# Attention prologue of a three-layer kernel: GpSimd starts after the ranking, VectorE subtracts for two heads at once, score tile 0 stands between the mask rows

## The chip, the cores and the metric

The kernel runs on one core of a Trainium2 chip. The metric is the time of one execution on the device, in microseconds (us). A profile is one further execution with the hardware profiler on; its times below count from the start of its span.

## The reference

Three layers in a row: clustered attention (batch 2, 8 heads, 768 positions, 64 columns a head, 16 clusters a head), then two feed-forward layers on its result. The change touches only the start of the attention.

```python
q_assign = argmax(einsum('bhsd,hcd->bhsc', q_n, c_n))   # 16 clusters a head, the first maximum wins
k_assign = argmax(einsum('bhsd,hcd->bhsc', k_n, c_n))
mask = q_assign[:, :, :, None] == k_assign[:, :, None, :]
scores = where(mask, (q @ k.T) / 8, -1e9)
attn = softmax(scores)                                   # then attn @ v
x = attention, heads side by side                        # 1536 x 512
h = x @ w_in;  g = rational(h);  y = g @ w_out           # 2048 hidden columns
logits = y @ phi; soft mixture of 8 experts (w1, relu, w2) over 32 slots
```

## The kernel before, in words

**Pairs and tiles.** Heads are handled in 8 pairs; a pair lies on 128 partitions, 64 for each head. A score tile is 128 queries of one head against all 768 keys, so a pair has 12 tiles and the attention 96. Tile u belongs to pair u // 12, and head u % 2. For each head of a pair four operands of 128 x 768 exist, `q1`, `q2`, `k1`, `k2` (the profile prints them as q and k): the inputs are split into a high part and a low rest (`qh` and `ql`, `ka` and `kb`) for accuracy, and 16 rows of `q2` and `k2` hold the cluster as one-hot mask rows. A tile is the sum of a first pass (`q1` against `k1`) and a second pass (`q2` against `k2`), each in two column halves (`a1_mm`, L361 and L362).

**The loop.** Slots n from -2 on; every engine runs its instructions in the order in which they are written, and a table `plan` puts each step of a pair's preparation, of a weight decoder and of the normalisation into a slot. Slot n does, for tile n + 2, the matmuls (`a1_mm`) and VectorE's pass that scales and takes the row minimum (`a1_neg`, L370); ScalarE's exponential (`a1_exp`, L374) follows one slot later. For tile n TensorE transposes (`turn`, L385) and ScalarE copies (`turned`, L391); matmuls with `v` follow six slots later (L398). In this text neg(u), exp(u), turn(u) and copy(u) are these steps of tile u. There is one PSUM buffer for the scores of tiles and one for the transposed ones.

**Preparation of a pair.** Cluster scores (`scores`, L240), scaled by the centroids' inverse norms `rn` (`scaled`, L245), transposed (`scT`, L250), then the ranking on VectorE: maximum (`mx`, L255), comparison (L257), first maximum by rank (L266, L268, L270), which leaves the one-hot tile `eq`. For pairs from 1 on GpSimd splits k (`ksplit`, tiles ka, kb) and q (`qsplit`, qh, ql), and SP copies the parts and the mask rows (`nh`, from ScalarE's `masks`, L280) into the operands by DMA: `mspread` is eight such DMAs (L288), `qspreads` six (L324).

**Pair 0** (`first_pair`) has its own code, before the loop. `front` writes high parts with ScalarE (q) and GpSimd (k), rests with VectorE and GpSimd, moves halves of them between partitions by DMA (`q_over`, `k_over`), and makes mask rows with TensorE's transposes of `eq` (`rows`, L182), VectorE (`q_rows`, L186) and ScalarE (`k_rows`, L190). `idle(n)` is n matmuls on zeros that nobody reads. `start` loads the centroids (`cP` for the norms, `cT` for the scores), q and k of pair 0 in two column halves, and the constants, and computes `rn` in a dozen small steps on VectorE with one on GpSimd (L495).

**Weight decoder.** `w_in` and `w_out` come as 64-bit numbers and are decoded beside the attention (`decode_steps`: load, `bits` L519 and L520, `expo` on ScalarE, `mant` L526, `sign` L530, `value` L535 and `parts` on GpSimd, `store`), at the slots in `DEC`. The feed-forward layers follow after the last tile; expert weights (`wt`) are loaded by SP as their buffers come free.

Of the kernel before, what the change touches and what calls it, by code (L numbers as in the profile page):

```python
# [52 lines left out]
def tile_kernel(ctx, tc, qT, kT, v, cenT, cenP, consts, constsb, ab, w_in, w_out, phi, w1, w2, out, dbg=None):  # L53
# [60 lines left out]
    PREP1 = (-2, 0, 0, 1, 1, 2, 1, 2, 3, 3, 4, 5, 6, 2, 3, 5, 7)  # L114
# [28 lines left out]
    def first_pair(r, o, f):  # L143
# [40 lines left out]
        def q_rows(h, c):
            a = slice(AT[h], AT[h] + 16)
            DVE.tensor_scalar(o[h]["q2"][a, halves[c]], ms["q", h][a, halves[c]], -1.0, None, ALU.add)  # L186

        def k_rows(h):
            a = slice(AT[h], AT[h] + 16)
            ACT.activation(o[h]["k2"][a, :], ms["k", h][a, 0:S], AF.Copy, scale=BIG)  # L190

        def front():
            f["scores"]()
            q_high(0)
            q_low(0, DVE)
# [17 lines left out]
            for h in range(2):  # L213
                rows("k", h)
                k_rows(h)
                rows("q", h)
                q_rows(h, 0)
# [3 lines left out]
                (0, "D", lambda: q_rows(0, 1)),  # L221
                (1, "D", lambda: q_rows(1, 1))]
# [128 lines left out]
    def a1_mm(u):  # L351
# [115 lines left out]
    def start():  # L467
        DVE.memset(zero, 0.0)
        idle(9)
        ACT.dma_start(cP, cenP)  # L470
        ACT.dma_start(cT, cenT)
        nc.scalar.preload_act_table_set("natural_log_exp_and_others")

        for n in "kq":
            raws.setdefault(0, {})[n] = raw_p.tile([128, S], F32, tag="raw" + n, name="raw" + n, bufs=2)
        for c in range(2):
            w = slice(c * HS, (c + 1) * HS)
            for n in "kq":
                SP.dma_start(raws[0][n][:, w], (kT if n == "k" else qT)[0, 0][:, w])
# [15 lines left out]
        POOL.tensor_scalar(t, r, 1e-6, 1.0, ALU.add, ALU.mult)  # L495
# [852 lines left out]
```

## Time and profile before

| | |
|---|---|
| time, median of 3 runs | 520.5 us (520.29 to 522.15) |
| the profiled execution | 519.72 us, of which 517.9 us are its span |
| TensorE busy | 499.2 us, 96% of the span, mean granted clock 0.994 |
| VectorE, ScalarE, GpSimd busy | 406.1, 366.2 and 280.3 us |
| span 0 to 16 us | TensorE busy 11.06, VectorE 9.65, ScalarE 7.04, GpSimd 11.38 us |
| span 48 to 265 us | TensorE busy 214.08 of 217 us |

The profiled execution is 1.8 us longer than its span, for what lies around it, and 0.8 us under the median. Busy shares are averages over stages: the attention fills the first half of the span, the two feed-forward layers the second.

### The profile page before, as it was taken

To read this page: it belongs to the slowest core of one execution; us is meant where nothing else is said; L and a number is where in the kernel's file an instruction comes from. 1 tells how busy PE (TensorE), PEld (TensorE's weight loads), DVE (VectorE), ACT (ScalarE), POOL (GpSimd) and SP (SyncE) were. 2 spreads that over 40 slices of the span, in tenths; PEclk is the share of its full clock that TensorE was granted. 3 is DMA by queue.
4 is the path that set the end of the run, shared out by engine and by line. 5 is a ranking of instruction groups with operands and counts; after the bars stand their busy time and mean duration, and the time that the engine had idled before them with its cause. 6 is when DMAs were issued, how large, how long until landed. Compare 5 with 4: busy or idle time off the path is not lost.

```text
span 517.9 us, 9816 instructions
## 1 busy us (share of the span) xinstructions
PE 499.2 (96%) x3439; PEld 336.2 (65%) x3439; DVE 406.1 (78%) x747; ACT 366.2 (71%) x653; POOL 280.3 (54%) x321
## 2 busy tenths in 40 slices
PE   6899999999999999999999999999999999999994
PEld 2656566666666666567666877777777767764462
DVE  6698899798998988988642999999799996985021
ACT  4577888788788887778773888879588786771111
POOL 6444876549676496665423855555355544641000
PEclk9899999999999999999999999999999999999999
DMA  6849889797986869773401767766567765799997
GB/s 198 243 135 271 259 219 320 220 259 216 265 292 175 285 203 295 240 212 130 164 1 64 259 232 264 276 226 224 185 223 253 263 216 195 271 352 378 422 414 307
DMA packets 43984, 124.61 MB, mean 241 GB/s; under 512 B 6944, under 2 KB 8992, under 8 KB 39328
## 3 DMA queue, kind: packets, MB, share of 16 engines
q1 hardware_dynamic: 43504, 123.54, 71.2%
q8 instruction: 27, 0.44, 0.4%
q10 hardware_dynamic: 432, 0.46, 0.3%
q14 instruction: 21, 0.17, 0.1%
HBM read 89.56 MB, written 15.73 MB: 203 GB/s over the span
## 4 chain that ended last, share of the span: by engine, by line
PE 70%; DVE 12%; DMA 9%; ACT 6%; issue 2%; POOL 1%; SPq 0%; ACTq 0%; POOLq 0%; DVEq 0%
PE sT L385 10%; PE av L398 10%; PE h L771 9%; PE h L774 9%; PE h L772 9%; DMA wt<-w 7%; PE s L361 5%; PE s L362 5%; DVE e L370 4%; PE gt L818 4%; ACT e L374 2%; ACT eT L391 2%; PE l L830 2%; PE dg L892 1%; DMA raw<-w_out 1%
## 5 line engine op out<-in xcount | busy, mean ns | idle before, releaser
L374 ACT ACTIVATE e<-e,nv 128x768 f32<-128x768 f32 x96 | 89.9, 937 | 44.1 <-DVE e L370 37.5
L370 DVE TENSOR_SCALAR_CACHE_REDUCE e<-s 128x768 f32<-128x768 f32 x96 | 91.5, 954 | 30.0 <-PE s L362 23.4
L385 PEld LDWEIGHTS sT<-cst,e 128*128 128x128 f32 x576 | 61.5, 141 | 45.5 <-ACT eT L391 24.6
L385 PE MATMUL sT<-cst,e 128*128 128x128 f32 x576 | 83.5, 281 | 2.2 <-ACT eT L391 1.7
L391 ACT COPY eT<-sT 128x768 f32<-128x768 f32 x96 | 75.4, 786 | 7.4 <-PE sT L385 6.8
L771 PE MATMUL h<-xh,w 128*128 128x512 f32 x192 | 80.6, 420 | 0.0
L535 POOL TENSOR_TENSOR w<-mh,ex 128x516 f32<-128x516 f32 x32 | 41.3, 1290 | 66.4 <-DVE ex L530 54.8
L398 PE MATMUL av<-eT,vt 128*64 128x384 f32 x384 | 77.2, 504 | 0.0
L788 POOL TENSOR_SCALAR q<-u,babs 128x512 f32<-128x512 f32 x47 | 36.5, 776 | 73.6 <-ACT u L786 73.6
L361 PE MATMUL s<-k,q 128*128 128x384 f32 x192 | 73.6, 384 | 2.1 <-DVE e L370 1.9
L772 PE MATMUL h<-xl,w 128*128 128x512 f32 x192 | 75.3, 392 | 0.0
L362 PE MATMUL s<-k,q 80*128 80x384 f32 x192 | 64.9, 338 | 0.0
L790 POOL TENSOR_TENSOR q<-q,u 128x512 f32<-128x512 f32 x47 | 61.0, 1299 | 3.8
L774 PE MATMUL h<-xh,w 128*128 128x512 f32 x192 | 52.9, 396 | 0.0
L786 ACT ACTIVATE u<-h 128x512 f32<-128x512 f32 x47 | 27.9, 594 | 27.2 <-PE h L774 23.6
L771 PEld LDWEIGHTS h<-xh,w 128*128 128x128 f32 x192 | 36.1, 188 | 16.3 <-DVE r L804 3.4
L789 DVE TENSOR_TENSOR p<-p,h 128x512 f32<-128x512 f32 x47 | 32.1, 683 | 15.0 <-ACT p L787 14.9
L774 PEld LDWEIGHTS h<-xh,w 128*128 128x128 f32 x192 | 35.9, 188 | 8.6 <-DMA w<-w_in 0.2
L361 PEld LDWEIGHTS s<-k,q 128*128 128x128 f32 x192 | 36.5, 190 | 6.6 <-DVE e L370 5.7
L772 PEld LDWEIGHTS h<-xl,w 128*128 128x128 f32 x192 | 36.2, 189 | 6.7 <-issue 0.5
L796 ACT ACTIVATE r<-q,epsc 128x512 f32<-128x512 f32 x47 | 32.8, 697 | 9.5 <-POOL q L790 7.5
L398 PEld LDWEIGHTS av<-eT,vt 128*64 128x64 f32 x384 | 21.4, 135 | 24.4 <-issue 22.7
(203 smaller groups left out, 956.3 us busy)
## 6 DMA issues: line engine op xcount, KB each, us to landing
wt<-w SPq DMA_DIRECT2D x32, 1024.0 KB, 8.2
w<-w_in SPq DMA_DIRECT2D x96, 256.0 KB, 3.3
raw<-w_in SPq DMA_DIRECT2D x16, 512.0 KB, 4.8
raw<-w_out SPq DMA_DIRECT2D x16, 512.0 KB, 4.7
w_in<-w SPq DMA_DIRECT2D x16, 512.0 KB, 4.4
k<-ka SPq DMA_DIRECT2D x28, 192.0 KB, 4.9
q<-qh SPq DMA_DIRECT2D x28, 192.0 KB, 4.7
w_out<-w SPq DMA_DIRECT2D x16, 256.0 KB, 4.9
```

What stands on the lines that cost most here:

```text
L361: PE.matmul(ps[:, c, 0:HS], o["q1"][:, it], o["k1"][:, w], start=True, stop=False)
L362: PE.matmul(ps[:, c, 0:HS], o["q2"][rows, it], o["k2"][rows, w], start=False, stop=True)
L370: DVE.tensor_scalar(e, s1s.pop(u)[:, :, 0:HS], -(D ** -0.5), None, ALU.mult, ALU.min, accum_out=nvs[g][:, rest:rest + 1])
L374: ACT.activation(es[u], es[u], AF.Exp, scale=-1.0, bias=nvs[g][:, rest:rest + 1], accum_out=sums[g][:, rest:rest + 1])
L385: PE.transpose(ps[:, j // 3, j % 3 * 128:(j % 3 + 1) * 128], e[:, j, :], ident)
L391: ACT.copy(dst, eTp.pop(u)[:, :, 0:HS].rearrange("p c (j t) -> p c j t", j=3))
L398: PE.matmul(av[g][64 * h:64 * h + 64, 0:HS], vs[g // 2][:, h, j, :], eTs[g][:, h, j, :], start=(j == 0), stop=(j == 5))
L535: POOL.tensor_tensor(w.rearrange("p (r n) -> p r n", r=3), hold["mh"].bitcast(F32), hold["ex"].bitcast(F32), ALU.mult)
L771: PE.matmul(h, wh[:, c, :], xh[t][:, c, :], start=(c == 0), stop=False)
L772: PE.matmul(h, wh[:, c, :], xl[t][:, c, :], start=False, stop=False)
L774: PE.matmul(h, wl[:, c, :], xh[t][:, c, :], start=False, stop=(c == NCC - 1))
L790: POOL.tensor_tensor(q, q, u, ALU.mult)
```

## The change

In `front`, ScalarE writes the high parts of q (first half) and of all of k to whole 128-partition tiles `qh` and `ka`; VectorE makes the rests `ql` and `kb` for both heads in one instruction each; ScalarE then writes the heads' own parts, and SP also carries `kb` to `k2` by DMA (`k_low`). GpSimd's first instruction after its memsets is a copy of one element of the finished `eq` (`gate`), so its work on q's second half starts after the ranking. The mask rows are made for q's first half only, before tile 0; its second half follows in slot 0. Tile 0's and tile 1's passes stand apart, between mask rows and pair 1's cluster scores. In `start`, SP issues the centroids `cP` first, ScalarE issues `cT` and q, SP k, and the GpSimd step of `rn` moves to VectorE. Pair 1's steps move in the slots (`PREP1`), the first decoder starts two slots earlier (`DEC`), and six of the idle matmuls go.

```diff
-    PREP1 = (-2, 0, 0, 1, 1, 2, 1, 2, 3, 3, 4, 5, 6, 2, 3, 5, 7)
+    PREP1 = (-1, 0, 1, 1, 2, 1, 3, 4, 4, 5, 5, 6, 2, 3, 6, 7)
...
+        def q_high(c, copy):
+            copy(hold["qh"][:, halves[c]], r["q"][:, halves[c]])
         def q_low(c, engine):
-            for h in range(2):
-                at = own[h], halves[c]
-                engine.tensor_tensor(hold["ql"][at], r["q"][at], o[h]["q1"][at].bitcast(F32), ALU.subtract)
+            w = halves[c]
+            engine.tensor_tensor(hold["ql"][:, w], r["q"][:, w], hold["qh"][:, w].bitcast(F32), ALU.subtract)
+        def q_own(n, h, c, copy):
+            copy(o[h][n][own[h], halves[c]], r["q"][own[h], halves[c]])
-        def k_high(h):
-            POOL.tensor_scalar(o[h]["k1"][own[h], :], r["k"][own[h], :], 1.0, 1.0, ALU.mult, ALU.mult)
+        def k_own(h):
+            ACT.copy(o[h]["k1"][own[h], :], r["k"][own[h], :])
         def k_low(h):
-            POOL.tensor_tensor(o[h]["k2"][own[h], :], r["k"][own[h], :], o[h]["k1"][own[h], :].bitcast(F32), ALU.subtract)
+            SP.dma_start(o[h]["k2"][own[h], :].bitcast(F32), hold["kb"][own[h], :].bitcast(F32))
...
-        def front():
+        def front(nxt):
             f["scores"]()
-            q_high(0)
+            q_high(0, ACT.copy)
+            ACT.copy(hold["ka"], r["k"])
             q_low(0, DVE)
-            k_high(0)
-            k_high(1)
+            DVE.tensor_tensor(hold["kb"], r["k"], hold["ka"].bitcast(F32), ALU.subtract)
+            k_over(0)
+            k_over(1)
             q_over(0, 0)
-            k_over(0)
+            k_low(0)
             q_over(1, 0)
-            k_over(1)
+            k_low(1)
             f["scaled"]()
             f["scT"]()
             f["best"](0)
             f["best"](1)
             for i in range(3):
                 f["first"](i)
-            q_high(1)
-            k_low(0)
-            k_low(1)
+            for h in range(2):
+                q_own("q1", h, 0, ACT.copy)
+                k_own(h)
+                q_own("q2", h, 0, ACT.copy)
+            pool_copy(s2_p.tile([128, 1], F32, tag="gate", name="gate"), hold["eq"][:, 2, 7, 15:16])
+            q_high(1, pool_copy)
             q_low(1, POOL)
+            for n in ("q1", "q2"):
+                for h in range(2):
+                    q_own(n, h, 1, pool_copy)
             idle(11)
-            for h in range(2):
-                rows("k", h)
-                k_rows(h)
-                rows("q", h)
-                q_rows(h, 0)
+            rows("q", 0, (0,))
+            rows("k", 0, (0, 1))
+            q_rows(0, 0)
+            k_rows(0)
+            a1_mm(0, (0,))
+            rows("q", 1, (0,))
+            q_rows(1, 0)
+            a1_mm(0, (1,))
+            rows("k", 1, (0, 1))
+            k_rows(1)
+            a1_mm(1, (0,))
+            nxt()
+            a1_mm(1, (1,))
...
-        idle(9)
-        ACT.dma_start(cP, cenP)
+        idle(8)
+        SP.dma_start(cP, cenP)
...
-            for n in "kq":
-                SP.dma_start(raws[0][n][:, w], (kT if n == "k" else qT)[0, 0][:, w])
+            SP.dma_start(raws[0]["k"][:, w], kT[0, 0][:, w])
+            ACT.dma_start(raws[0]["q"][:, w], qT[0, 0][:, w])
...
-        POOL.tensor_scalar(t, r, 1e-6, 1.0, ALU.add, ALU.mult)
+        DVE.tensor_scalar(t, r, 1e-6, None, ALU.add)
...
-    DEC = [2 + 53 * i // 20 for i in range(2 * NF)]
+    DEC = [2 * (i > 0) + 53 * i // 20 for i in range(2 * NF)]
...
-            if n > 0 or n == -LEAD:
+            if n >= 0:
                 a1_mm(pend)
             a1_neg(pend)
-            if n < 0:
-
-                a1_mm(n + 1 + LEAD)
...
-        if n < 6 and n != -1:
-            idle(2 if n < 0 else 3)
+        if 0 < n < 6:
+            idle(3)
```

GpSimd, from its last memset to the first work for pair 1. Before, it makes the norm's step, then high parts and rests of pair 0 (rawk and rawq are the inputs, k_0_0 and q_0_0 operands of head 0, k_0_1 and q_0_1 of head 1):

```order
L495 TENSOR_SCALAR pc<-pc 128x4
L167 TENSOR_SCALAR k_0_0_118<-rawk 64x768
L167 TENSOR_SCALAR k_0_1_122<-rawk 64x768
L170 TENSOR_TENSOR k_0_0_119<-rawk,k_0_0_118 64x768
L170 TENSOR_TENSOR k_0_1_123<-rawk,k_0_1_122 64x768
L161 TENSOR_TENSOR ql<-rawq,q_0_0_116 64x384
L161 TENSOR_TENSOR ql<-rawq,q_0_1_120 64x384
L293 TENSOR_SCALAR ka<-rawk 128x768
```

Now the copy out of `eq` stands first, and only q's second half follows before pair 1's ka:

```order
L177 TENSOR_SCALAR gate<-eq 128x1
L177 TENSOR_SCALAR qh<-rawq 128x384
L159 TENSOR_TENSOR ql<-rawq,qh 128x384
L177 TENSOR_SCALAR q_0_0_116<-rawq 64x384
L177 TENSOR_SCALAR q_0_1_120<-rawq 64x384
L177 TENSOR_SCALAR q_0_0_117<-rawq 64x384
L177 TENSOR_SCALAR q_0_1_121<-rawq 64x384
L318 TENSOR_SCALAR ka<-rawk 128x768
```

All of k's work has left this place, and nothing of GpSimd's runs while VectorE ranks.

TensorE, from the last mask row of before to the transposes of tile 1 (s is a score tile, mf the cluster scores, sT the transposed tile, rest the idle matmuls; rows that repeat are left out):

```order
L182 MATMUL mb<-cb,eq 16x128
L361 MATMUL s_276<-k_0_0_118,q_0_0_116 128x384
L362 MATMUL s_276<-k_0_0_119,q_0_0_117 128x384
...
L361 MATMUL s_285<-k_0_1_122,q_0_1_120 128x384
L362 MATMUL s_285<-k_0_1_123,q_0_1_121 128x384
...
L240 MATMUL mf<-rawq,cT 32x384
...
L465 MATMUL rest<-zero 128x512
...
L361 MATMUL s_302<-k_0_0_118,q_0_0_116 128x384
...
L385 MATMUL sT<-cst,e 128x128 x6
L250 MATMUL mf<-cst,sc 128x128 x3
```

Now, from the first score pass on:

```order
L392 MATMUL s_262<-k_0_0_118,q_0_0_116 128x384 x2
...
L187 MATMUL mb<-cb,eq 16x128
...
L390 MATMUL s_262<-k_0_0_119,q_0_0_117 128x384 x2
...
L392 MATMUL s_278<-k_0_1_122,q_0_1_120 128x384 x2
L265 MATMUL mf<-rawq,cT 32x384
...
L390 MATMUL s_278<-k_0_1_123,q_0_1_121 128x384 x2
L418 MATMUL sT<-cst,e 128x128 x6
L392 MATMUL s_315<-k_0_0_118,q_0_0_116 128x384
```

Tile 0's two passes now enclose q's rows of head 1, tile 1's enclose pair 1's cluster scores, and tile 2 (s_302 before, s_315 now) follows turn(0) in place of preceding it.

ScalarE, from tile 0's exponential on (sc is pair 1's scaled cluster scores, eT the copy of a transposed tile). Before:

```order
L374 ACTIVATE e,ssum<-e,nv 128x768 x2
L391 COPY eT<-sT 128x6x128
L245 ACTIVATE sc<-mf,pc 128x384
L374 ACTIVATE e,ssum<-e,nv 128x768
L391 COPY eT<-sT 128x6x128
```

Now:

```order
L407 ACTIVATE e,ssum<-e,nv 128x768
L270 ACTIVATE sc<-mf,pc 128x384
L407 ACTIVATE e,ssum<-e,nv 128x768
L424 COPY eT<-sT 128x6x128
L407 ACTIVATE e,ssum<-e,nv 128x768
```

The scaling for pair 1 has moved from behind copy(0) to ahead of exp(1). On SP's queue the store of the first decoded weights, which stood between pair 1's eight mask-row DMAs and its six q DMAs, now stands ahead of both. From tile 6 on VectorE's instructions stand in the same order in both kernels, and so do the other engines' from a few tiles later to the end.

## Rows read from the trace of the kernel before

**Rows 1.** The chain of waits near the span's end: start, duration in us, what.
```profile
472.49 15.93 DMA wt<-w
```
**Rows 2.** Timeline of SP's queue near the end: start, us, engine, line, operation, tiles.
```profile
446.19 42.63 SPq L751 DMA_DIRECT2D wt<-w  x21
```
**Rows 3.** Timeline of the prologue, all engines; brackets: idle before, and what ended it.
```profile
7.25 0.20 POOL L495 TENSOR_SCALAR pc<-pc 128x4 f32<-128x4 f32 x1 [3.54 <-DVE pc L494]
...
7.57 2.28 DVE L161 TENSOR_TENSOR ql<-rawq,q 64x384 fp32r<-64x384 f32 x2
7.75 0.58 ACT L245 ACTIVATE sc<-mf,pc 128x384 f32<-128x384 f32 x1 [1.11 <-DVE pc L496]
8.23 2.09 ACT L154 CAST q<-rawq 64x384 fp32r<-64x384 f32 x4
...
8.77 2.54 PE L465 MATMUL rest<-zero 128*128 128x512 bf16 x11
...
9.53 3.87 POOL L170 TENSOR_TENSOR k<-rawk,k 64x768 fp32r<-64x768 f32 x2
9.89 0.56 DVE L255 TENSOR_REDUCE mx<-mf 128x24 f32<-128x384 f32 x1
...
11.07 0.66 DVE L266 TENSOR_TENSOR eq<-eq,cb 128x384 bf16<-128x384 bf16 x1
...
12.35 1.46 DVE L270 TENSOR_TENSOR eq<-eq,mr 128x384 bf16<-128x384 bf16 x1
...
13.86 2.49 PE L182 MATMUL mb<-cb,eq 128*16 128x128 bf16 x24 [2.55 <-DVE eq L270]
...
14.71 1.69 ACT L190 ACTIVATE k<-mb 16x768 fp32r<-16x768 bf16 x2 [4.39 <-PE mb L182]
...
17.64 0.96 DVE L370 TENSOR_SCALAR_CACHE_REDUCE e<-s 128x768 f32<-128x768 f32 x1 [0.69 <-PE s L362]
...
18.52 0.95 DVE L370 TENSOR_SCALAR_CACHE_REDUCE e<-s 128x768 f32<-128x768 f32 x1
```
**Rows 4.** The same timeline later, while GpSimd has nothing to do.
```profile
25.91 0.35 DVE L266 TENSOR_TENSOR eq<-eq,cb 128x384 bf16<-128x384 bf16 x1
...
28.84 0.55 DVE L270 TENSOR_TENSOR eq<-eq,mr 128x384 bf16<-128x384 bf16 x1
...
29.80 0.34 PE L275 MATMUL mb<-cb,eq 128*128 128x128 bf16 x3
...
32.11 1.29 POOL L535 TENSOR_TENSOR w<-mh,ex 128x516 f32<-128x516 f32 x1 [13.40 <-DVE ex L530]
```
**Rows 5.** Groups by line of VectorE, 17 to 34 us: busy us, mean ns.
```profile
L370 DVE TENSOR_SCALAR_CACHE_REDUCE e<-s 128x768 f32<-128x768 f32 x7 | 6.6, 954 | 1.4 <-PE s L362 1.0 <-ACT eT L391 0.4
L519 DVE TENSOR_SCALAR ex<-raw 128x516 int32<-128x516 int32 x2 | 1.4, 682 | 0.0
...
L186 DVE TENSOR_SCALAR q<-mb 16x384 fp32r<-16x384 bf16 x2 | 1.1, 552 | 0.1
```
**Rows 6.** Windows: busy of five engines, then granted clock, DMA share, GB/s.
```profile
13.00:13.50 0.50, 0.00 (x0) 0.00 (x0) 0.50 (x1) 0.00 (x0) 0.42 (x2) 1.00 0.83 318
...
14.00:14.50 0.50, 0.50 (x7) 0.50 (x6) 0.00 (x0) 0.00 (x0) 0.50 (x1) 0.50 0.65 262
```
**Rows 7.** Timeline of TensorE in slot 0: pair 1's cluster scores transposed.
```profile
22.35 0.55 PE L250 MATMUL mf<-cst,sc 128*128 128x128 f32 x3 [1.37 <-ACT sc L245]
```
**Rows 8.** Timeline of VectorE: neg(6).
```profile
33.15 0.94 DVE L370 TENSOR_SCALAR_CACHE_REDUCE e<-s 128x768 f32<-128x768 f32 x1
```
**Rows 9.** Timeline: last q DMA of pair 1, and tile 12's first matmul.
```profile
43.08 0.60 SPq L324 DMA_DIRECT2D q<-qh  x1
...
48.19 0.44 PE L361 MATMUL s<-k,q 128*128 128x384 f32 x1 [0.21 <-DVE e L370]
```
**Rows 10.** DMA issues between 5 and 14 us: KB each, median us to landing.
```profile
k<-k SPq DMA_DIRECT2D x2, 192.0 KB, 2.8
```
**Rows 11.** Instructions on the tiles k, 15 to 50 us: their DMAs' landing.
```profile
DMA to landing us min/median/max: 1.8/4.8/7.8
```

More of the change, by code (lines that the diff above doesn't have):

```diff
@@ L149, in first_pair, with temp @@
         ms = {}
-        def q_high(c):
-            for n in ("q1", "q2"):
-                for h in range(2):
-                    ACT.copy(o[h][n][own[h], halves[c]], r["q"][own[h], halves[c]])
+        def temp(n):
+            hold[n] = t_p.tile([128, S], F32R, tag=n, name=n)
+        def q_high(c, copy):
+            copy(hold["qh"][:, halves[c]], r["q"][:, halves[c]])
         def q_low(c, engine):
-            if c == 0:
-                hold["ql"] = t_p.tile([128, S], F32R, tag="ql", name="ql")
-            for h in range(2):
-                at = own[h], halves[c]
-                engine.tensor_tensor(hold["ql"][at], r["q"][at], o[h]["q1"][at].bitcast(F32), ALU.subtract)
+            w = halves[c]
+            engine.tensor_tensor(hold["ql"][:, w], r["q"][:, w], hold["qh"][:, w].bitcast(F32), ALU.subtract)
@@ L176, in rows @@
+        def rows(name, h, cs):
             g = 2 * (name == "k") + h
-            m = ms[name, h] = m_tile(BF16)
+            if name not in ms:
+                ms[name] = m_tile(BF16)
             oh = hold["eq"].rearrange("p i (c g) n -> p i c g n", c=2)
-            for c in range(2):
+            for c in cs:
                 for i in range(3):
                     j = (3 * c + i) * 128
-                    PE.transpose(m[AT[h]:AT[h] + 16, j:j + 128], oh[:, i, c, g, :], identb)
+                    PE.transpose(ms[name][AT[h]:AT[h] + 16, j:j + 128], oh[:, i, c, g, :], identb)
@@ L349, in tile_kernel, with a1_mm @@
     nvs, sums, s1s, es = {}, {}, {}, {}
-    def a1_mm(u):
+    def a1_mm(u, passes=None):
         p, idx = divmod(u, 12)
@@ L357, in a1_mm, with one @@
         rows = slice(0, (80, 128)[h])
-        ps = s1s[u] = psS[u == 1].tile([128, 2, 512], F32, tag="S", name="s1")
-        for c in range(2):
+        if u not in s1s:
+            s1s[u] = psS[u == 1].tile([128, 2, 512], F32, tag="S", name="s1")
+        ps = s1s[u]
+        def one(c, second):
             w = slice(c * HS, (c + 1) * HS)
-            PE.matmul(ps[:, c, 0:HS], o["q1"][:, it], o["k1"][:, w], start=True, stop=False)
-            PE.matmul(ps[:, c, 0:HS], o["q2"][rows, it], o["k2"][rows, w], start=False, stop=True)
+            if second:
+                PE.matmul(ps[:, c, 0:HS], o["q2"][rows, it], o["k2"][rows, w], start=False, stop=True)
+            else:
+                PE.matmul(ps[:, c, 0:HS], o["q1"][:, it], o["k1"][:, w], start=True, stop=False)
+        for c, second in ((0, 0), (0, 1), (1, 0), (1, 1)) if passes is None else [(c, i) for i in passes for c in range(2)]:
+            one(c, second)
     def a1_neg(u):
@@ L640, in tile_kernel @@
     front, rest = prep(0)
-    front()
+    steps = prep(1)
+    front(steps.pop(0)[2])
     add(0, rest)
-    for slot, (_, eng, fn) in zip(PREP1, prep(1)):
+    for slot, (_, eng, fn) in zip(PREP1, steps):
         plan.setdefault(slot, {}).setdefault(eng, []).append(fn)
```

25 lines of the change are left out of this document (14 added, 11 removed).

## Prediction

> **What bounds the kernel now.** I read the page's busy shares first: TensorE is at 96% over the span, but only 11.06 of the first 16 us, so what the change touches is a stage in which TensorE waits. All later work hangs on how early the first score tiles are done, if nothing downstream runs on a clock of its own. The chain of waits ends in a load of expert weights [rows 1], which could be such a clock. SP's queue speaks against it: the last 21 loads start to be issued at 446.19 us [rows 2], each into a buffer that a TensorE step has given back, so the stream starts when TensorE arrives and moves with it. From tile 6 on the two programs hold the same instructions in the same order. A gain at tile 6 should therefore reach the end whole.
>
> The timeline of the prologue shows the chain in order [rows 3]. Centroid norms end at about 7.66 (the reciprocal behind the GpSimd step of 7.25). VectorE then subtracts twice, 2.28 us for two 64x384 pieces, and only then starts mx at 9.89, with no idle time before it: VectorE itself is late, not the scores. The ranking ends at 12.35 + 1.46 = 13.81, TensorE turns 24 mask rows in 2.49 us, and neg(0) starts at 17.64, neg(1) at 18.52.
>
> Two things in it are dearer than later. The same ranking steps take 0.66 and 1.46 us here, beside GpSimd's subtractions [rows 3], and 0.35 and 0.55 us at 25.91 and 28.84, when GpSimd had been idle for long (13.40 us before its next work at 32.11) [rows 4]. And TensorE, idle from 11.31 to 13.86, still had its full clock in the half microsecond from 13.0, and half of it (1.2 GHz) in the one from 14.0 [rows 6]: the rows go at 2.49 / 24 = 0.104 us each, against 0.34 / 3 = 0.11 at most for full-width transposes at 29.80 with one latency in it [rows 4]; taking 0.2 us of that as latency leaves some 0.06 each.
>
> **The change, part by part.** All from the profiled execution (519.72 us, 0.8 under the median).
>
> Norms: the hop to GpSimd and back (7.16, where the step of 7.00 ends, to 7.48) becomes a VectorE step of 0.17; 0.08 us gained, rn at 7.58.
>
> Subtractions: one 128x384 instead of two 64x384, at 0.55 (the two-input step of that width at 28.84 with GpSimd idle [rows 4]), and a new one, 128x768, at 0.95 (VectorE's pass of that width [rows 5]). 7.58 + 0.55 + 0.95 + gaps gives mx at 9.13, not 9.89. Its scores must be there: the scaling waits for rn (7.67 to 8.25), the transposes take 0.55 [rows 7], 8.85, so they are. ScalarE's two new copies come before the scaling and have from q's and k's landing to 7.67 for 0.5 + 0.85. If GpSimd were not the cause of the slow pair, ql and kb would cost double, mx would start at 10.6 and the term would be a loss of 0.7; the rows at 25.91 and 28.84 speak against that.
>
> Ranking: mx and its comparison 0.56 each, then 0.35, 0.55, 0.55 and gaps: 2.7 us, end at 11.83 in place of 13.81. **Gain 1.98.**
>
> Mask rows to neg(0): the eleven idle matmuls end 0.1 earlier, at 11.2, so TensorE waits 0.65 us, not 2.55, and I take the full clock. Three rows of q and six of k end at 12.45; ScalarE's six copies for the operands (2.09 / 4 = 0.52 each for 64x384, 1.69 / 2 = 0.85 for 768 columns of k [rows 3]) end at 11.95, so k's rows are copied 12.6 to 13.4 (0.80). Head 1's q rows wait for VectorE's 0.55 [rows 5] inside that time, and tile 0's first pass is done in it. The second pass then needs 0.35 plus a handoff: neg(0) at 13.95. Before, 3.83 us lay between the ranking's end and neg(0), now 2.12. **Gain 1.7**, 3.7 in all. Tile 1 waits for k's rows of head 1 (14.25 to 15.05) and stands behind pair 1's cluster scores: neg(1) at 15.75, 2.8 earlier.
>
> First slots: exp(0) stands behind the second k_rows, 15.1 to 16.05; turn(0), then tile 2: neg(2) about 18.05, behind two decoder steps of 0.68 [rows 5] that have moved here. Before, pair 1's scaling stood behind copy(0) on ScalarE, and TensorE waited for it 1.37 us at 22.35, with turn(1) behind [rows 7]. Now it stands ahead of exp(1), and the transposes are due near 18.1. What sets the pace next is VectorE's list: neg(2), mx, comparison and a decoder step (0.95 + 0.56 + 0.56 + 0.69 and gaps) put neg(3) at 20.95; three negs, three ranking steps, two q_rows, three decoder steps (2.9 + 1.45 + 1.1 + 2.05 and gaps) put neg(6) at 28.7. It was at 33.15 [rows 8]. **Gain 4.4 at neg(6)**, where the programs become equal. Of it 3.7 is from the parts above, 0.7 from the order. VectorE's list can meet GpSimd's splits of pair 1's q again near 27; one step at the contended price costs 0.9. Between none and 0.9, and since a list by hand misses handoffs, I take off 0.5: **3.9 us**.
>
> Idle matmuls: six fewer take nothing from the path; they lay beside waits.
>
> Loads: `cP` was already first in its queue; k, q and cT are issued up to 0.45 us sooner because two queues issue. By these rows the norms gain nothing, since they wait for cP alone; I take 0. The Trainium skill (DMA: Bandwidth & Descriptors, Issuing engines are not separate DMA queues) says that several issuing engines share the same 16 DMA engines and save only issue time. By it, too, the sum stays at 3.9, and the words "load first" buy nothing; no row here shows cP alone in front of the engines.
>
> GpSimd: its list for pair 0 held k's high parts, 3.87 us of rests and q's half; with pair 1's k split behind it, it was done at 32.11 - 13.40 = 18.7 [rows 4]. Now it starts at about 11.9 and holds one gate (0.2, as the step of 7.25), a split of 1.5, four copies of 0.5 and pair 1's k (2.85), so it is done near 18.5. Twice the price for q's part would make that 3.5 us later. What waits there is SP with ka's DMAs, and behind them the first decoder's store and pair 1's mask rows, not needed before 32; GpSimd had 13.40 us idle before 32.11 [rows 4], which is the cover.
>
> SP: pair 1's mask rows wait for ScalarE's masks, which now follow exp(6) and a decoder step, at about 32.9; before they were sent from 33.5. So the six q DMAs end only some 1.3 us earlier than 43.08 + 0.60 [rows 9], while tile 12 (48.19 [rows 9]) wants to start 4 us earlier. Head 1's last DMA, issued at 41.8 with a landing of 4 to 4.8 (the median of [rows 11]), is there at 46.6; tile 13, one slot after tile 12, wants it at 47. That is the thinnest cover of the change.
>
> Sum: 519.72 - 3.9 = 515.8 for a profiled execution, 520.5 - 3.9 = 516.6 for the median.
>
> **The rivals.** (Chances at the end; a measurement of this kernel tells about 0.5%, 2.6 us, from no change.)
>
> The clock falls all the same. TensorE has small waits between mask rows and passes, and fewer idle matmuls. At 0.104 for a row and doubled passes neg(0) comes at 14.6, neg(1) at 16.8: gain 3.0, 517.5. For it: the rows at 14.0 [rows 6]. Against: 2.2 us of idleness (11.31 to 13.5) had not lowered it in these rows, and the longest wait now is 0.65. The Trainium skill (TensorE: Matmul & The Clock Gate, What's actually happening) has throttling as the default state that activity lifts; a rule that speaks against taking idle matmuls out, and with it this rival's 517.5.
>
> Pair 1's operands come late. If the last q DMAs land like the longest of the k tiles, 7.8 [rows 11], tile 13 waits until 49.6, 2.6 us past its wish: gain 1.3 to 1.6, 518.9. For it: the median there is 4.8, above what I assume for the quiet stretches. Against: a 512 KB store has left the place just ahead of these DMAs.
>
> Nothing reaches the end. If the weight stream [rows 1] were bound by its own rate from its start, or some load early in the span were, the early gain would pile up as a wait: 520.5. Against: rows 2.
>
> Slower: k's low part arrives late. GpSimd wrote it in place by 13.4 (9.53 + 3.87 [rows 3]); now it goes by DMA behind VectorE's kb, issued at 9.15 and 10.3 for the two heads, and the second passes wait for it. At 2.8 [rows 10] it lands at 12.0 and 13.1, 1.5 and 2 us before need. At 7.8 tile 0 starts at 17.0 and the gain shrinks to nothing at neg(1); from about 8.5 us on the kernel is slower, at 10 us by about 1.3: 521.8. Against: that price was paid in a fuller stretch.
>
> **How the numbers follow.** Forecast (gain 3.0 to 4.7) 0.55, its own range 515.8 to 517.5; clock 0.13; late operands 0.15; nothing arrives 0.09; slower, by this or by another way, 0.08. Faster by over 0.5%: 0.55 + 0.13 = 0.68; within 0.5%: 0.15 + 0.09 = 0.24; slower: 0.08. The range goes from a gain of 5.2 (the 4.4 without discount, and 0.8 for a decoder step behind neg(6) that meets GpSimd no more, as 1.46 against 0.55 above) to 519.6, beyond the late operands; it leaves out the slower case, most of "nothing arrives" and a little below.
>
> **What would show it.** Right: ql near 0.55 and kb near 0.95 us; the three last ranking steps at 0.35, 0.55, 0.55; eq done near 11.8; a granted clock of 1.00 through 12 to 16 us; neg(0) near 14, neg(3) near 21, neg(6) near 29; tile 12 near 44 with no wait for a DMA. Wrong: any DMA named before tiles 0, 1, 12 or 13; a clock of 0.5 after 13 us; a gap before the last weights that was not there.

## The result, and the profile after

The changed kernel takes 516.13 us (median of 5 executions, 514.81 to 516.5) against 520.5 (5 executions, 519.0 to 522.15). The ratio is 0.9908, 95% interval 0.988 to 0.9935: 4.4 us faster, the forecast having been 516.6. The profiled execution took 514.81 us, its span is 513.0.

VectorE's timeline of the prologue after the change (start, us, engine, line, operation, tiles; brackets: idle before, and what ended it):

```profile
3.15 0.43 DVE L518 TENSOR_TENSOR csq<-cP 128x256 f32<-128x256 f32 x1 [2.02 <-DMA cP<-cenP]
...
6.59 0.55 DVE L159 TENSOR_TENSOR ql<-rawq,qh 128x384 fp32r<-128x384 f32 x1
7.06 0.95 DVE L204 TENSOR_TENSOR kb<-rawk,ka 128x768 fp32r<-128x768 f32 x1
8.43 0.56 DVE L280 TENSOR_REDUCE mx<-mf 128x24 f32<-128x384 f32 x1 [0.41 <-PE mf L275]
...
9.61 0.36 DVE L291 TENSOR_TENSOR eq<-eq,cb 128x384 bf16<-128x384 bf16 x1
10.00 0.55 DVE L293 TENSOR_REDUCE mr<-eq 128x24 bf16<-128x384 bf16 x1
10.59 0.56 DVE L295 TENSOR_TENSOR eq<-eq,mr 128x384 bf16<-128x384 bf16 x1
...
13.42 0.96 DVE L403 TENSOR_SCALAR_CACHE_REDUCE e<-s 128x768 f32<-128x768 f32 x1
...
15.72 0.96 DVE L403 TENSOR_SCALAR_CACHE_REDUCE e<-s 128x768 f32<-128x768 f32 x1 [1.34 <-PE s L390]
```

Before, the middle one of the last three ranking steps was this line, beside the two in [rows 3]:

```profile
11.77 0.55 DVE L268 TENSOR_REDUCE mr<-eq 128x24 bf16<-128x384 bf16 x1
```

Read the timeline against [rows 3]. The pair of subtractions is 1.5 us instead of 2.28 for ql alone, the last three ranking steps cost 0.36, 0.55 and 0.56 instead of 0.66, 0.55 and 1.46, and the ranking ends at 10.59 + 0.56 = 11.15 instead of 13.81. VectorE now has 0.41 us of idleness ahead of mx: TensorE's transposes are late, not VectorE. neg(0) starts at 13.42 (17.64), but neg(1) only 2.3 us behind it, having waited 1.34 for TensorE; before it followed after 0.88.

TensorE's timeline of the same stretch, and two of its windows (busy of five engines, granted clock, DMA share, GB/s):

```profile
8.23 2.54 PE L498 MATMUL rest<-zero 128*128 128x512 bf16 x11
11.20 0.67 PE L187 MATMUL mb<-cb,eq 128*16 128x128 bf16 x9 [0.44 <-DVE eq L295]
...
13.31 0.50 PE L187 MATMUL mb<-cb,eq 128*16 128x128 bf16 x6
...
15.07 0.62 PE L390 MATMUL s<-k,q 128*128 128x384 f32 x2
16.84 0.85 PE L418 MATMUL sT<-cst,e 128*128 128x128 f32 x6 [1.15 <-DVE e L403]
```

```profile
13.00:14.00 1.00, 1.00 (x9) 0.64 (x9) 0.93 (x2) 0.09 (x1) 0.92 (x2) 1.00 0.64 254
14.00:15.00 1.00, 1.00 (x10) 0.20 (x9) 0.39 (x2) 0.97 (x2) 0.86 (x3) 1.00 0.61 146
```

The wait ahead of the mask rows is 0.44 us, not 2.55; the granted clock is 1.00 where it was 0.50 in [rows 6]; nine rows take 0.67. The 1.15 us ahead of turn(0) matter too: tile 1's scores lie in the buffer of the transposed tiles, so it waits until neg(1) has read them.

The rest of the way, in the timelines of VectorE, SP and TensorE and, in the last row, the chain of waits:

```profile
26.54 0.88 DVE L295 TENSOR_TENSOR eq<-eq,mr 128x384 bf16<-128x384 bf16 x1
...
28.54 0.94 DVE L403 TENSOR_SCALAR_CACHE_REDUCE e<-s 128x768 f32<-128x768 f32 x1
```

```profile
41.01 0.71 SPq L349 DMA_DIRECT2D q<-qh  x1
...
43.53 0.45 PE L392 MATMUL s<-k,q 128*128 128x384 f32 x1 [0.22 <-DVE e L403]
...
46.55 0.42 PE L392 MATMUL s<-k,q 128*128 128x384 f32 x1
...
441.54 42.67 SPq L780 DMA_DIRECT2D wt<-w  x21
```

```profile
467.89 15.93 DMA wt<-w
```

neg(6) is 4.61 earlier than in [rows 8], tile 12's first matmul 4.66 earlier than in [rows 9], the last stream of weights 4.65 and the load at the chain's end 4.60 earlier than in [rows 2] and [rows 1]. What was won by tile 6 reaches the end whole. The span is 4.9 shorter; the further 0.3 arises behind that last load and is not explained here.

Part of the difference of the medians may be clock lost elsewhere. Of 57 executions of the kernel before that were timed beside the experiments, the 11 with a mean granted clock of 0.989 or less have a median of 521.8 us and the 16 with 0.995 or more one of 519.2; the five of the kernel after lie between 0.995 and 0.998. Against executions of a like clock the gain would be nearer to 3 us than to 4.4: an estimate, 519.2 - 516.13, from medians that were not taken side by side. Where those executions lost their clock is not recorded.

### The profile page after: what moved, and what is told of

Its sections match the earlier page's. It is cut to its first block, busy times and chain, and to the rows that moved or that the text cites. A ratio compares the mean times of both kernels' runs of the same rounds, so it can differ in the third digit from the quotient of the medians.

```text
span 513.0 us, 9820 instructions
## 1 busy us (share of the span) xinstructions
PE 497.2 (97%) x3433; PEld 334.1 (65%) x3433; DVE 403.2 (79%) x748; ACT 367.3 (72%) x653; POOL 275.8 (54%) x321
## 4 chain that ended last, share of the span: by engine, by line
PE 66%; DVE 11%; DMA 10%; ACT 5%; SPq 3%; issue 2%; POOL 1%; ACTq 0%; DVEq 0%
PE h L800 9%; PE sT L418 9%; PE h L803 9%; PE av L431 9%; PE h L801 9%; DMA wt<-w 7%; DVE e L403 5%; PE s L392 4%; PE s L390 4%; PE gt L847 4%; ACT e L407 2%; PE l L859 2%; ACT eT L424 2%; DMA w_in<-w 1%; PE dg L921 1%
```

## The experiments

Each run changes the kernel after, except two that change the kernel before. In all, the same landmarks are read: the ranking's end (start and duration of its last step), neg(0), neg(1), neg(6), and the span, in us of one profiled execution each.

| kernel | ranking ends | neg(0) | neg(1) | neg(6) | span |
|---|---|---|---|---|---|
| before | 13.81 | 17.64 | 18.52 | 33.15 | 517.9 |
| after | 11.15 | 13.42 | 15.72 | 28.54 | 513.0 |
| e1, no gate | 12.07 | 14.33 | 16.65 | 29.41 | 514.6 |
| e2, cP on ScalarE's queue | 11.87 | 15.12 | 17.43 | 30.24 | 516.2 |
| e3, scaling behind copy(0) | 12.16 | 15.56 | 17.86 | 31.07 | 515.8 |
| e4, no idle matmuls | 12.48 | 15.99 | 19.78 | 32.60 | 517.6 |
| e5, q DMAs later | 11.33 | 13.60 | 15.90 | 28.74 | 520.3 |
| e6, before with cP first | 12.90 | 15.79 | 16.68 | 31.30 | 516.3 |
| e7, a subtraction a head | 12.38 | 14.65 | 16.96 | 29.79 | 514.7 |
| e8, pair 1 loaded late | 11.24 | 17.66 | 21.22 | 34.04 | 519.7 |
| e9, idle matmuls in a wait | 11.59 | 13.86 | 16.17 | 28.99 | 514.1 |
| e10, rows, then passes | 10.83 | 14.26 | 16.17 | 28.98 | 514.0 |
| e11, before with idle(20) | 13.44 | 16.34 | 17.22 | 31.84 | 515.6 |
| e12, tile 1 first | 12.78 | 17.14 | 18.17 | 30.99 | 517.3 |

(e5 is the kernel after up to tile 11.) Between kernels with the same instructions up to the cluster scores (after, e3, e4, e5, e9, e10, e12) the ranking's end differs by up to 1.95 us, mostly with the landing of raw q; in e4 also because all eight matmuls of the cluster scores took 0.82 to 0.85 us, where the last four took 0.49 to 0.51 in the kernel after. So distances between landmarks are compared, not the landmarks alone.

**e1_no_gate**

```diff
-            pool_copy(s2_p.tile([128, 1], F32, tag="gate", name="gate"), hold["eq"][:, 2, 7, 15:16])
```

> The changed kernel without the one-element copy out of eq, so GpSimd starts on q's second half as soon as that has landed (about 6.3 us). Theory (GpSimd's work makes VectorE's two-input steps dear): ql rises from 0.55 to about 1.1 us and kb from 0.95 to about 1.8, mx starts near 9.8 in place of 8.43, the two two-input ranking steps cost 0.66 and 1.0 to 1.4, the ranking ends near 13.2 in place of 11.15, neg(0) comes near 15.3 in place of 13.42, neg(6) 1.3 to 2 us later than 28.54, and the time is about 1.5 us above that of the changed kernel. Rival (the steps were slow for another reason, for instance because they came in halves of 64 partitions): all durations as in the changed kernel, ranking end at 11.2, no change of the time.

516.67 us (10 executions) against 520.85; ratio 0.9938, 0.9911 to 0.9963. VectorE's timeline:

```profile
6.65 1.34 DVE L159 TENSOR_TENSOR ql<-rawq,qh 128x384 fp32r<-128x384 f32 x1
7.91 1.25 DVE L204 TENSOR_TENSOR kb<-rawk,ka 128x768 fp32r<-128x768 f32 x1
...
10.25 0.64 DVE L290 TENSOR_TENSOR eq<-eq,cb 128x384 bf16<-128x384 bf16 x1
```

With GpSimd at work beside them the same steps cost 1.34, 1.25 and 0.64 instead of 0.55, 0.95 and 0.36, and the ranking ends 0.92 later. The slow steps are a matter of what GpSimd does at that moment. neg(6) comes 0.87 later, less than the 1.3 to 2 expected, since the last step of the ranking met no GpSimd work in this run: GpSimd had run into a wait of 1.88 us for the DMA that carries pair 0's kb away. The ratio does not tell this kernel from the kernel after (0.988 to 0.9935); the trace does.

**e2_cp_other_queue**

```diff
-        SP.dma_start(cP, cenP)
-        ACT.dma_start(cT, cenT)
+        ACT.dma_start(cP, cenP)
+        SP.dma_start(cT, cenT)
```

> The changed kernel with cP issued first by ScalarE and cT first by SP, so the same two loads are the first ones, on the other queue each. Before, cP landed 3.3 us after its issue at 0.73 and the norms began at 4.05; after the change, 2.4 us and 3.15. Theory (what is issued beside cP in the same half microsecond shares the DMA engines: 192 KB of k before, 64 KB of cT now): the norms begin near 3.15 again. Rival (it is SP's queue that is served sooner than ScalarE's): they begin near 4.05, rn ends near 7.6, mx starts near 9.1 and neg(0) near 14.0.

The norms began at 3.22, as in the kernel after (3.15): which of the two queues carries cP does not matter here. The run lost time elsewhere. TensorE waited 1.07 us for raw q between the halves of the cluster scores, and its timeline goes on:

```profile
6.83 0.51 PE L265 MATMUL mf<-rawq,cT 128*32 128x384 f32 x1 [1.07 <-DMA rawq<-qT]
...
8.90 4.07 PE L498 MATMUL rest<-zero 128*128 128x512 bf16 x11
12.91 0.67 PE L187 MATMUL mb<-cb,eq 128*16 128x128 bf16 x9
```

One of its windows:

```profile
10.00:11.00 1.00, 1.00 (x3) 0.30 (x2) 0.93 (x3) 1.00 (x2) 0.00 (x0) 0.50 0.77 218
```

The granted clock was 0.50 from 9 to 12 us, so the idle matmuls took 4.07 us instead of 2.54, and the mask rows, which stood behind them, began 1.04 after the ranking. From neg(1) to neg(6) it is again 12.81.

**e3_sc_behind_copy**

```diff
-    PREP1 = (-1, 0, 1, 1, 2, 1, 3, 4, 4, 5, 5, 6, 2, 3, 6, 7)
+    PREP1 = (0, 0, 1, 1, 2, 1, 3, 4, 4, 5, 5, 6, 2, 3, 6, 7)
```

> The changed kernel with pair 1's scaling one slot later, behind exp(1) and copy(0) on ScalarE, as before the change. As the prediction had it, the order of the first slots gave 0.7 us at neg(6). Theory: scaling near 18.6 in place of 15.80, pair 1's transposes near 19.2 with TensorE waiting for them, turn(1) near 19.8 in place of 18.97, neg(3) 0.4 to 0.8 us later than 21.04 and neg(6) as much later than 28.54. Rival (VectorE's list hides it): neg(6) within 0.2 us of 28.54.

TensorE's timeline of slot 0 shows it waiting again for the scaling, less than the 1.37 of [rows 7]:

```profile
21.25 0.55 PE L275 MATMUL mf<-cst,sc 128*128 128x128 f32 x3 [0.46 <-ACT sc L270]
```

neg(1) to neg(6) takes 13.21 instead of 12.82: the step is worth 0.39. (Its idle matmuls took 4.21 us at the low clock, as in e2, after a wait of 1.02 for raw q; hence its late neg(0).)

**e4_no_idle_matmuls**

```diff
-            idle(11)
```

> The changed kernel without the eleven idle matmuls between the cluster scores and the mask rows, so TensorE stands still from 8.4 to 11.2 us. Theory (the full clock through the mask rows was worth part of the gain): the granted clock is at half after about 11 us, the nine mask rows take about 0.95 us in place of 0.67 and the passes up to twice as long, neg(0) comes 0.4 to 0.6 us and neg(1) 0.8 to 1.2 us later, neg(6) about 0.5 us later than 28.54. Rival: the clock stays at full and nothing moves.

TensorE's timeline, and one window with the granted clock third from the end:

```profile
12.53 1.13 PE L187 MATMUL mb<-cb,eq 128*16 128x128 bf16 x9 [2.81 <-DVE eq L294]
13.59 1.01 PE L391 MATMUL s<-k,q 128*128 128x384 f32 x2
```

```profile
13.00:14.00 1.00, 1.00 (x8) 0.79 (x6) 0.56 (x1) 0.30 (x1) 0.92 (x2) 0.50 0.97 354
```

TensorE idled 2.81 us, the granted clock stood at 0.50 in the next window, rows and passes cost 1.13 and 1.01 instead of 0.67 and 0.62. From the ranking's end neg(0) is 3.51 away (2.27 in the kernel after), neg(6) 20.12 (17.39): 2.7 us, where 0.5 was expected, because the low clock lasted past tile 1.

**e5_q_dmas_later**

```diff
-    PREP1 = (-1, 0, 1, 1, 2, 1, 3, 4, 4, 5, 5, 6, 2, 3, 6, 7)
+    PREP1 = (-1, 0, 1, 1, 2, 1, 3, 4, 4, 5, 5, 6, 2, 3, 6, 8)
```

> The changed kernel with pair 1's six q DMAs one slot later, so that on SP they stand behind a decoder load, v's load and a store. Theory (these DMAs are the thinnest cover, and a loss at tile 12 is not made good later): they are issued from about 44.7 in place of 37.6, tile 12 waits for them until about 49 to 50 in place of 43.53, tile 13 until about 52, and the time rises by 4 to 6 us over the changed kernel, to that of the kernel before or above it. Rival (later slots have slack that takes it up): the same wait at tile 12, but the time rises by less than half of it.

521.79 us (10 executions) against 519.99; ratio 1.0032, 1.001 to 1.0054; span 520.3. One slot later for six DMAs undoes the whole change. TensorE's timeline, tile 12:

```profile
47.77 0.66 PE L392 MATMUL s<-k,q 128*128 128x384 f32 x1 [4.26 <-DMA q<-ql]
```

Up to neg(11) nothing moved; neg(12) came 4.6 and neg(13) 6.9 later, and the span's end 7.3. Not all of that is the wait itself: with it the granted clock fell, and it stood at 0.50 from 48 to 52 us.

**e6_before_cp_first** (the kernel before)

```diff
-        ACT.dma_start(cP, cenP)
+        SP.dma_start(cP, cenP)
         ACT.dma_start(cT, cenT)
```

> The kernel before with only the centroids first: SP issues cP ahead of k and q, ScalarE issues cT. Theory (the norms were late because cP shared the engines with k, and the whole early chain hung on them): the norms begin near 3.2 in place of 4.05, VectorE's subtractions near 6.7 in place of 7.57, the ranking ends near 12.95 in place of 13.81, neg(0) comes near 16.8 in place of 17.64, neg(6) near 32.3 in place of 33.15. Rival (q and k, issued 0.4 us later now, hold the chain): the subtractions start early, but mx waits for the scores, and neg(0) moves by less than 0.3 us.

VectorE's timeline:

```profile
3.15 0.43 DVE L487 TENSOR_TENSOR csq<-cP 128x256 f32<-128x256 f32 x1 [2.02 <-DMA cP<-cenP]
...
6.66 2.28 DVE L161 TENSOR_TENSOR ql<-rawq,q 64x384 fp32r<-64x384 f32 x2
```

And TensorE's first mask rows:

```profile
12.96 0.96 PE L182 MATMUL mb<-cb,eq 128*16 128x128 bf16 x18 [2.16 <-DVE eq L270]
```

Against the profile of the kernel before, this one line brings the norms and the ranking's end 0.9 us forward, with the slow subtractions as they were. (Against e11, the other profile with the old order of loads, it is 0.5.) neg(0) gained more, 1.85: TensorE idled 2.16 us ahead of the rows (2.55 in [rows 3]) and kept a granted clock of 1.00.

**e7_subtract_by_head**

```diff
-            engine.tensor_tensor(hold["ql"][:, w], r["q"][:, w], hold["qh"][:, w].bitcast(F32), ALU.subtract)
+            for h in range(2):
+                engine.tensor_tensor(hold["ql"][own[h], w], r["q"][own[h], w], hold["qh"][own[h], w].bitcast(F32), ALU.subtract)
...
```

> The changed kernel with VectorE's two subtractions cut into one for each head again (64 partitions each, four instructions). Theory (the time goes by columns, not by partitions, and stands on the path): 0.55 twice and 0.95 twice, mx near 9.4 in place of 8.43, ranking end near 12.15 in place of 11.15, neg(0) near 14.4, neg(6) 0.7 to 1.0 us later than 28.54. Rival (hidden: mx has 0.41 us of idle time before it and TensorE's list sets neg(1)): neg(6) within 0.3 us.

VectorE's timeline, the subtractions of q and, edited in the same way, of k:

```profile
6.52 1.13 DVE L160 TENSOR_TENSOR ql<-rawq,qh 64x384 fp32r<-64x384 f32 x2
7.68 1.94 DVE L206 TENSOR_TENSOR kb<-rawk,ka 64x768 fp32r<-64x768 f32 x2
```

Two instructions of 64 partitions cost twice one of 128. The ranking ends 1.23 later, neg(6) 1.25.

**e8_pair1_load_late** (pair 1's k and q are loaded by SP behind `k_over`, not in `start`)

```diff
+            for n in "kq":
+                r1[n] = raw_p.tile([128, S], F32, tag="raw" + n, name="raw" + n, bufs=2)
+                SP.dma_start(r1[n], (kT if n == "k" else qT)[0, 1])
             q_over(0, 0)
...
-        load(1, "k")
-        load(1, "q")
```

> The changed kernel with pair 1's q and k loads (384 KB each) issued behind the first two k DMAs of pair 0, at about 7.8 us in place of 3.3. Theory (they share the DMA engines with the last of pair 0's q and k, and since the norms end early it is those that the scores wait for): q's second half lands near 5.6 in place of 6.3, the scaling starts near 6.75 (rn's end) in place of 7.21, mx near 8.05 (behind kb) in place of 8.43, neg(6) 0.3 to 0.4 us earlier; pair 1's inputs land near 13, just before TensorE asks for them. The time falls by 0.4 us, less than the timing can tell. Rival: pair 1's inputs come too late, TensorE waits for them at 14 us, and neg(1) and neg(6) are later.

521.52 us (10 executions) against 519.99; ratio 1.0015, 0.998 to 1.005. Pair 0's scores were scaled no earlier (7.30, after 7.21), and the loss is not at pair 1:

```profile
15.29 0.98 PE L395 MATMUL s<-k,q 128*128 128x384 f32 x2 [3.33 <-DMA q<-ql]
```

The two loads, issued from 8.00 to 9.09, stood ahead of `q_over` of pair 0, and tile 0's first pass waited 3.33 us for it. Behind that wait the granted clock was 0.50 from 14 to 20 us, and with the slower passes neg(6) lost 5.5 in all. That is near to the prediction's slower rival: a part of pair 0 that travels by DMA comes late, here q's, which did so in the kernel before too. In the kernel after no pass of pair 0 waits for a DMA.

**e9_idle_in_scaling_wait**

```diff
             f["scaled"]()
+            idle(3)
             f["scT"]()
```

> The changed kernel with three idle matmuls put on TensorE between the cluster scores and their transposes, where it waits 0.71 us for ScalarE's scaling in every run so far. Theory (in the runs in which raw q's second half landed late, TensorE paused twice, 1.0 us and 0.7 us, the granted clock fell to 0.50 near 9 us, the eleven idle matmuls took 4.1 us instead of 2.54 and ended about 1 us after the ranking): the three fill the second pause, the clock stays at 1.00 from 8 to 16 us whenever q lands, neg(0) stands 2.2 to 2.4 us behind the ranking's end, and the median is no higher than the changed kernel's 516.1, the slower executions being fewer. Rival A: one pause of 1.0 us is enough by itself and the clock still falls near 9 us when q is late. Rival B: the three matmuls end after the scaling and put the transposes, and all that follows, 0.1 to 0.3 us later, with nothing won.

515.70 us (6 executions, 514.6 to 516.38) against 519.48; ratio 0.9931, 0.9911 to 0.9951. The granted clock was 1.00 throughout and ranking to neg(0) took 2.27. But the wait between the halves of the scores was 0.48 us in this profile, not the 1.0 that it was meant to guard against, so the guard was not put to the test by it; rival B did not happen beyond 0.1 us. Inconclusive.

**e10_rows_then_passes**

```diff
+            rows("q", 1, (0,))
+            q_rows(1, 0)
+            rows("k", 1, (0, 1))
+            k_rows(1)
             a1_mm(0, (0,))
-            rows("q", 1, (0,))
-            q_rows(1, 0)
             a1_mm(0, (1,))
-            rows("k", 1, (0, 1))
-            k_rows(1)
```

> The changed kernel with TensorE's order undone: all 18 mask rows first, then both passes of tile 0. Nothing else moves (the other engines' lists are the same but for buffer numbers). Theory (the order is worth little by itself, the clock and the earlier ranking carry the gain): the 18 rows take 1.2 to 1.4 us, both passes 1.2, neg(0) stands 2.6 to 2.7 us behind the ranking's end instead of 2.27; but the second k_rows on ScalarE can follow the first at once (13.5 instead of 14.7 at its end), so neg(1) is no later than 15.7, neg(6) moves by less than 0.3, and the median stays within 0.5 of 516.1. Rival (the order carries its part of the 1.7 us of the prediction): neg(0) 0.6 to 0.9 later and neg(6) with it, 516.7 to 517.

515.78 us (9 executions) against 519.48; ratio 0.9938, 0.9915 to 0.9962: the medians do not tell it from the kernel after, the trace does. TensorE's timeline:

```profile
11.86 0.33 PE L187 MATMUL mb<-cb,eq 128*16 128x128 bf16 x3 [0.31 <-DVE q L191]
12.44 0.49 PE L187 MATMUL mb<-cb,eq 128*16 128x128 bf16 x6 [0.25 <-ACT k L195]
12.86 0.61 PE L392 MATMUL s<-k,q 128*128 128x384 f32 x2
```

The second rows wait until the first have been copied out of their buffer, a wait that the interleaved order covers with a pass. neg(0) is 3.43 behind the ranking's end instead of 2.27, neg(6) 18.15 instead of 17.39. The theory fell; the rival (the order carries its own part) was right, with 0.76 us.

**e11_before_more_idle** (the kernel before)

```diff
-            idle(11)
+            idle(20)
```

> The kernel before with twenty idle matmuls instead of eleven behind the cluster transposes, so that TensorE pauses for about half a microsecond before the mask rows instead of 2.55 us. Theory (the clock is a part of the 1.7 us between ranking end and neg(0)): granted clock 1.00 through 13 to 17 us, 24 mask rows in about 1.5 us instead of 2.49, neg(0) 2.7 to 2.9 us behind the ranking's end instead of 3.83, neg(6) about 1 us earlier, 519.5. Rival (the order, not the clock): neg(0) still 3.4 us or more behind the ranking's end, at a full clock. If the idle matmuls run at the low clock they overrun the ranking's end; then it tells nothing.

TensorE's timeline:

```profile
13.51 0.96 PE L182 MATMUL mb<-cb,eq 128*16 128x128 bf16 x18 [0.62 <-DVE eq L270]
14.90 0.49 PE L182 MATMUL mb<-cb,eq 128*16 128x128 bf16 x6 [0.43 <-ACT k L190]
```

The granted clock stayed at 1.00, the 24 rows took 1.45 us of work instead of 2.49. Ranking to neg(0) is 2.90 instead of 3.83, ranking to neg(6) 18.40 instead of 19.34: the clock alone is worth 0.94 us, in the kernel before, for nine matmuls that nobody reads. e6, with the old eleven and a clock of 1.00 as well, has 2.89 and 18.40, so it is the clock and not the number of idle matmuls that counts.

**e12_tile1_before_scores**

```diff
-            a1_mm(0, (1,))
             rows("k", 1, (0, 1))
             k_rows(1)
+            a1_mm(0, (1,))
             a1_mm(1, (0,))
-            nxt()
             a1_mm(1, (1,))
+            nxt()
```

> The changed kernel with the second group of k's mask rows (and ScalarE's copy of them) ahead of tile 0's second pass, and pair 1's cluster scores behind tile 1 instead of between its two passes. In the changed kernel and its variants so far neg(1) stands 4.57 us behind the ranking's end, in the kernel before at a full clock only 3.78, and from neg(1) to neg(6) all variants with the changed order of first slots take the same 12.8 us. Theory (neg(1) sets the pace after the change, since turn(0) waits for the score buffer that neg(1) frees): neg(0) 2.6 to 2.8 us behind the ranking's end, 0.4 later than now, but neg(1) 3.6 to 3.9, neg(2) 0.6 to 0.9 earlier against the ranking's end, and neg(6) 16.5 to 16.9 behind the ranking's end instead of 17.39; a median of 515.3 to 515.6 by that. Rival A (the pace is set from neg(0), or by exp(0) behind the second copy of k's rows): neg(6) 17.4 to 17.8, no gain. Rival B (pair 1's scaling, with scores that end later, becomes what VectorE waits for): neg(2) earlier but neg(3) not.

515.41 us (6 executions, 513.78 to 519.07) against 520.77; ratio 0.9903, 0.9878 to 0.9927. The profiled execution was its slowest: raw q came late, and the idle matmuls overran the ranking, as TensorE's timeline shows:

```profile
7.17 0.59 PE L265 MATMUL mf<-rawq,cT 128*32 128x384 f32 x1 [1.46 <-DMA rawq<-qT]
...
9.81 4.76 PE L498 MATMUL rest<-zero 128*128 128x512 bf16 x11
14.50 0.67 PE L187 MATMUL mb<-cb,eq 128*16 128x128 bf16 x9
```

Counted from the first mask row (14.50 here, 11.20 after), neg(0) is 2.64 away instead of 2.22, neg(1) 3.67 instead of 4.52, neg(6) 16.49 instead of 17.34: 0.85 us won at neg(1), and all of it still there at neg(6). The late start of the rows does not make the difference: in e2, where they were late too, the three distances are 2.21, 4.52 and 17.33. The theory holds in the trace, though two things were moved at once (k's rows and pair 1's scores) and their shares are not separated. As a time the version has the lowest median of all, but its interval overlaps that of the kernel after (0.988 to 0.9935), so it is not shown to be faster.

## Why the prediction was right, point by point

**What bounds it.** A gain at tile 6 reaches the end: 4.61 at neg(6), 4.60 at the chain's last load. Right; "nothing reaches the end" is out.

**Loads: "I take 0".** This step failed. The norms began 0.90 earlier. (The forecast had it that all of k, q and cT are issued sooner; k's first half is issued 0.44 later, at 1.18.) Issues in the kernels before and after (KB each, median us from issue to landing):

```profile
rawq<-qT SPq DMA_DIRECT2D x2, 192.0 KB, 3.6
cP<-cenP ACTq DMA_DIRECT2D x1, 128.0 KB, 3.3
```

```profile
rawq<-qT ACTq DMA_DIRECT2D x2, 192.0 KB, 4.3
cP<-cenP SPq DMA_DIRECT2D x1, 128.0 KB, 2.4
```

`cP` had been first in its queue before, but beside the 192 KB of k on the other; now 64 KB of `cT` go beside it, and k and q follow. e6 shows the gain by that line alone, e2 that it is not the queue. Its size is less sure than 0.9. e11, the other profile with the old order, has cP landing after 2.9 us and its norms beginning here:

```profile
3.69 0.42 DVE L487 TENSOR_TENSOR csq<-cP 128x256 f32<-128x256 f32 x1 [2.57 <-DMA cP<-cenP]
```

In the twelve profiles with the new order cP lands after 2.2 to 2.5 us and the norms begin at 3.01 to 3.24, so the gain lies between 0.45 and 1.04. That it comes from the bytes issued beside cP is what is left, not a thing that was measured by itself. The Trainium skill (DMA: Bandwidth & Descriptors, Issuing engines are not separate DMA queues) says that all issuing engines share the same DMA engines; e2 agrees (3.22 against 3.15). The forecast took from its rows that nothing is gained since the norms wait for cP alone; they do, but cP itself landed sooner. q lost: 4.3 us instead of 3.6 (3.5 in e6, where SP still issues it). So the scores became what VectorE waits for (0.41 ahead of mx), and of the 0.9 some 0.7 are left at mx: 8.43, forecast 9.13.

**Subtractions.** ql 0.55 and kb 0.95, as forecast. Both heads in one instruction are worth 1.23 (e7, kb's two included). The old pair took 2.28 beside GpSimd, the same pair in e7, with GpSimd idle, 1.13.

**Ranking, 1.98.** It ends 2.66 earlier. The mechanism was right: in the kernel after, GpSimd's absence is worth 0.9 us (e1) and the joining of the subtractions 1.2 (e7). The size was off by 0.68, and mx, which the loads brought forward, was already 0.70 early; from mx to the end it took 2.72 us, forecast 2.70.

**Mask rows to neg(0), 1.7.** 1.56 (2.27 instead of 3.83; forecast 2.12). Both named causes are real: the clock is worth 0.94 (e11, in the kernel before), and at a full clock the new order, with half of q's rows put off, still saves 2.90 - 2.27 = 0.63 at neg(0).

**The order of the first slots, 0.7.** 0.39, from neg(0) to neg(6) 15.12 instead of 15.51. The place of pair 1's scaling alone accounts for as much (e3). The rest was lost at tile 1: its second pass stands behind pair 1's cluster scores and its k rows behind tile 0's second pass, and e12 wins 0.85 by turning both round. The forecast had neg(1) at 15.75 and it came at 15.72, though the ranking ended 0.68 earlier: that is where the extra gain of the loads went.

**Discount of 0.5.** GpSimd did meet a ranking step (0.88 at 26.54, 0.33 too dear), inside the bounds, though mostly with the decoder's subtraction (25.73 to 27.01) and not with q's split, which began at 26.98. 2.66 + 1.56 + 0.39 = 4.61, where 3.9 was forecast. The undiscounted 4.4 was nearer by luck: 0.68 too little for the ranking stands against 0.14 too much for the mask rows and 0.31 too much for the order.

**GpSimd and SP.** kb of pair 1 was ready at 18.2 (forecast 18.5). The last q DMA was issued at 41.01 (41.8); landings there took 2.6 to 5.2 us, so it was there by 46.2 at the latest, and tile 13 started at 46.55 without a wait. "The thinnest cover" is the right name: e5 costs 7.3 us of span for one slot. k's low part of pair 0, the slower rival, was issued at 8.52 and 9.75, and no pass waited for it.

**The clock falls all the same.** Not in the profile of the kernel after, but in those of e2, e3 and e12, by a way that the rival did not have: not small waits among mask rows, but a late raw q earlier on. There the granted clock fell between 7 and 9.5 us, and the mask rows, behind idle matmuls that had been put in to hold it, began 1.0 to 1.7 us after the ranking. In the three, TensorE had waited 1.02 to 1.46 us between the halves of the scores; in the kernel after and e5, where the clock stayed, it waited there under 0.6. The Trainium skill (TensorE: Matmul & The Clock Gate, What's actually happening) has the low clock as the default that activity lifts; these runs agree (in e2 it was 0.50 from 9 to 12 us and 1.00 again from 12, with the idle matmuls running). That the late q is the cause was not tried by itself, and how often it happens in executions whose trace was not kept stays open: the mean clock of an execution does not tell it (0.994 in e2's profile, 0.995 in that of the kernel after). The rival was also priced too low: a low clock from the mask rows to tile 1 cost 2.7 us at neg(6) in e4, where the forecast took 3.9 - 3.0 = 0.9.

## What to carry to other kernels

Look at what is under way beside a critical load, not only at its place in its own queue. Put work of GpSimd that shares no data with a VectorE chain behind that chain, by a dependence if need be, and check what then comes late. When a wait goes, read which engine is late next: here the gain at tile 0 was partly handed back at tile 1, and only the distance between two landmarks showed it.

## What the runs showed of the hardware

A VectorE step that takes 0.17 us by itself took 0.37 beside GpSimd (the norm's addition in e1), and large two-input steps up to 1.46 where they take 0.55 alone ([rows 3, 4]). The same start-up code gave ranking ends 1.95 us apart from run to run, for the most part with the landing of 192 KB of q. After TensorE had been without work, its granted clock was still 1.00 behind 2.16 us of idleness in e6, and 0.50 in the window behind 2.55 in [rows 3, 6] and 2.81 in e4; but in e12 it was 0.50 from 7.5 us, behind a wait of only 1.46, so the length of the last wait does not decide it alone. The column of the granted clock reads 1.00 from the span's start in every profile, while the first idle matmuls of the kernel after take 3.59 / 8 = 0.45 us each and the later eleven 2.54 / 11 = 0.23: at the start it is the durations that tell the clock.
